# Decode backward, last pass: V and dS two blocks ahead of dV, dK and dQ

## The chip, the cores and the metric

One core of a Trainium2 chip runs the whole program in one launch. The metric is the device time of one execution in microseconds (us). A kernel's time is the median of several executions; beside it stands one execution that the hardware profiler recorded, and every duration below comes from that one.

## The reference

One token passes through four layers: attention over a cache of 65,536 keys and values (32 query heads in 4 groups of 8, head size 128), a feed-forward layer with squared ReLU, and both once more with the same weights and the same cache. The result and the gradients of all inputs but the feed-forward layer's own x are returned, so also the gradients of the K and V caches (4 x 65,536 x 128 each, bf16, 67 MB each).

```python
q = (x @ wq).reshape(...)                       # x: one token, layer-normed
scores = einsum("bhqd,bhkd->bhqk", q, k) * Dh ** -0.5
o = einsum("bhqk,bhkd->bhqd", softmax(scores), v)
A = o.reshape(...) @ wo                          # x = x + A(ln(x))
B = relu(ln(x) @ w1 + b1) ** 2 @ w2 + b2         # x = x + B
...
x = x + A(ln(x)); x = x + B(ln(x)); x = x + A(ln(x)); x = x + B(ln(x))
# returned: x and vjp(grad_out) for x, K, V, wq, wo, w1, b1, w2, b2
```

Both attention layers use the same K and V. So the gradient of one value row is a sum over two layers and eight heads, P^T dO, and that of a key row is dS^T q over the same sixteen pairs, where dS = P * (dO V^T - delta).

## The kernel before, in words

The caches are read in four passes: forward of layer 1, forward of layer 3, backward of layer 3 alone (dS and dQ), and a last pass, `attn_bwd4`, that works for both layers at once. Between the passes stand stages with the dense weights. The change concerns the last pass, which begins at about 1236 us of the profile and lasts to its end.

**Blocks and steps.** A block is 4096 keys of one head group as a tile of 128 partitions x 32 columns x 128 (`J` = 32): 1 MB in bf16. There are 64 blocks, 16 for each of the four groups. A step is an eighth of 64 columns, 8 columns of 128 keys; a block has four steps, the pass 256. `pipeline(items, stages, bg, end)` writes the steps out: in loop step i, a stage with lag l works on item i - l. In the last pass the order in which the engines get the instructions is not written out by hand: the framework's scheduler orders each engine's queue, with the order of the code as priority. Each engine then works through its queue in order.

**The stages of the last pass.** `vT` (lag 0) asks for the V block, transposes eight 128x128 pieces on TensorE (L1226) and copies them from PSUM (tile `kt`). The first seven V blocks were left in the arena, transposed, by the pass before and need neither. `vT` also copies the probabilities of both layers for the block into one tile, `xin`, on GpSimd (L1233). `vS` (lag 2) sets up a group or a unit of 128 columns (`g_setup`, `su_setup`), transposes `xin` (L1239), and forms dO V^T - delta in one PSUM tile (L1256 for delta, L1259 for the eight products). At the end of a block VectorE multiplies by the probabilities (X, L1267: this is dS), and TensorE transposes X at once (L1239). `dV8` (lag 3) makes the V gradient from the transposed probabilities, `k8` (lag 7) asks for the K block, adds K's part of dQ (L1306) and makes the K gradient from the transposed X. Both gradients go through `outer16`: pairs of TensorE products (L1280), a copy from PSUM into a slot (`evac`, L150 on ScalarE or L153 on VectorE, by estimated load), and a store from GpSimd's queue (L1286).

**Slots.** All K and V blocks, weight slabs and outgoing gradients live in the arena: 20 slots of 1 MB, of which 12 are free for this at the pass's start while 8 hold the probabilities of the four groups and two layers; two more come free when a group is done (`E_done`). Which slot each piece gets is fixed when the program is written out. For a load of the last pass, `take_one` picks

```python
early = [i for t, i in by_age if t <= NOW["step"] - AHEAD]   # AHEAD = 9
i = early[-1] if early else by_age[0][1]
```

and for an outgoing piece the youngest slot given back at least one step before. A stored slot counts as given back five steps later. Loads go out on the sync queue (L330 for K and V, L424 for weight slabs), which works in order and waits for each slot's last user.

**Around the steps.** `Background.step` runs one piece per step of the weight gradients (`g_outer`, `g_outer_wide`, products at L1345, stores at L1363), spread over the first 252 steps, and of the row products that give dO of the next group and the gradient of the layer's input (weight slabs of wo and wq, L549 and L540). The `end` list fetches the last V blocks and the last wq slabs at fixed distances from the loop's end. After the loop come the last group's row product and its part of dWq.

Of the kernel before, what the change touches and what calls it, by code (L numbers as in the profile page):

```python
# [10 lines left out]
BF = mybir.dt.bfloat16  # L11
# [5 lines left out]
P = 128  # L17
# [3 lines left out]
def kernel(  # L21
# [24 lines left out]
    nc = tc.nc  # L46
# [6 lines left out]
    R = HQ // G  # L53
# [3 lines left out]
    J = 32  # L57
    NB = C // J
    SU = min(128, C)
# [5 lines left out]
    R2, R4 = 2 * R, 4 * R  # L65
    TLEAD = 2
# [9 lines left out]
    tmp = ctx.enter_context(tc.tile_pool(name="tmp", bufs=2))  # L76
# [88 lines left out]

    def col_from_dram_f(v1d, n, name):
        nj = n // P
        rows = tmp.tile([nj // 4, 4 * P], BF, name="rows_f", tag="rows_f", bufs=1)
        nc.sync.dma_start(out=rows[:], in_=v1d.rearrange("(s x) -> s x", x=4 * P))
        pt = ps_mv([P, 4, 8], BF)  # L170
        col = vec.tile([P, nj // 4, 4], F32, name=name)
        for j in range(4):
            nc.tensor.transpose(pt[:, j, 0:nj // 4], f_cols(rows, j), ident_b[0:nj // 4, 0:nj // 4])
            nc.vector.tensor_copy(out=col[:, :, j], in_=pt[:, j, 0:nj // 4])
        return col[:, :, :].rearrange("p s j -> p (s j)")

    def col_to_dram_f(col, n, v1d):
        nj = n // P
        rows = tmp.tile([nj // 4, P, 4], BF, name="rows_f", tag="rows_f", bufs=1)
        c3 = col[:, :].rearrange("p (s j) -> p s j", j=4)  # L180
        for j in range(4):
            pt = ps_mv([nj // 4, P], F32)
            nc.tensor.transpose(pt[:, :], c3[:, :, j], ident_f[:, :])
            nc.vector.tensor_copy(out=rows[:, :, j], in_=pt[:])
        nc.gpsimd.dma_start(out=v1d.rearrange("(s x) -> s x", x=4 * P), in_=rows[:].rearrange("s p j -> s (p j)"))

    def col_to_dram(col, n, v1d):
        nj = n // P
# [184 lines left out]

    FWD_LAG = TLEAD + SU // 8 + 18
    B3_LAG = TLEAD + HB // 8 + 3
    B4_LAG = TLEAD + J // 8 + 1
    DV_LAG = TLEAD + 1
    ITEMS = [order_by_unit(False, SU), order_by_unit(True, SU), order_by_unit(False, HB), order_by_unit(True, J)]
    TOUCH = [touch_order(ITEMS[0], [("k", 0), ("v", FWD_LAG)]), touch_order(ITEMS[1], [("k", 0), ("v", FWD_LAG)]),
             touch_order(ITEMS[2], [("v", 0), ("k", B3_LAG)]), touch_order(ITEMS[3], [("v", 0), ("k", B4_LAG)])]  # L380
# [788 lines left out]
    def attn_bwd4(p, La, Lb, on_group, bg, stack, end=()):  # L1169
        dspool = stack.enter_context(tc.tile_pool(name="b4_ds", bufs=2))  # L1170
        items = ITEMS[p]
# [14 lines left out]
        def g_setup(g):  # L1186
            sl = gsl(g)
            for i, L in enumerate((La, Lb)):
                nc.vector.tensor_copy(out=DOB[:, g, 0, i * R:(i + 1) * R], in_=L["dOT"][:, sl])
                nc.vector.scalar_tensor_tensor(out=CCf[:, g, 0, i * R:(i + 1) * R], in0=L["qT"][:, sl], scalar=SCALE, in1=L["rZ"][:, sl],  # L1190
                                               op0=ALU.mult, op1=ALU.mult)
                nc.vector.tensor_tensor(out=CCf[:, g, 1, i * R:(i + 1) * R], in0=L["dOT"][:, sl], in1=L["rZ"][:, sl], op=ALU.mult)
            ndt = dspool.tile([64, J, R2], BF, name="ndt4", tag="ndt4", bufs=1)
            for i, L in enumerate((La, Lb)):
                nc.vector.tensor_copy(out=ndt[:, :, i * R:(i + 1) * R], in_=L["nd2"][:, sl].unsqueeze(1).to_broadcast([64, J, R]))
            state["ndt"] = ndt

        def su_setup(g, su):
# [19 lines left out]
        def vT(g, c8):  # L1218
            bg.need(g)
            vb8 = kv8("v", g, c8)  # L1220
            if is_turned("v", g, c8):
                state[("vt", g, c8)] = vb8
            else:
                pt = ps_tr()
                for i in range(8):
                    nc.tensor.transpose(pt[:, i, :], vb8[:, i, :], ident_b[:, :])  # L1226
                kv_done("v", g, c8)
                vt = turned_to("v", g, c8, vb8)
                evac(vt[:, :, :], pt[:, :, :])
                state[("vt", g, c8)] = vt  # L1230
            if c8 % J == 0:
                xin = dspool.tile([P, J, R2], BF, name="xin", tag="xin", bufs=1)
                nc.gpsimd.tensor_copy(out=split2(xin[:, :, :]), in_=E2(g, c8, J))  # L1233
                state[("xin", g, c8 // J)] = xin

        def x_transpose(src):
            pt = ps_tr()
            for bi in range(J // 8):
                nc.tensor.transpose(pt[:, bi, :], src[:, 8 * bi:8 * bi + 8, :].rearrange("p a b -> p (a b)"), ident_b[:, :])  # L1239
            xt = dspool.tile([P, J // 8, P], BF, name="xt", tag="xt", bufs=4)  # L1240
            evac(xt[:, :, :], pt[:, 0:J // 8, :])
            return xt

        def vS(g, c8):
            if c8 == gfirst[g]:
                g_setup(g)
            if c8 == sufirst[(g, c8 // SU)]:
                su_setup(g, c8 // SU)
            if c8 % J == 0:
                state[("xe", g, c8 // J)] = x_transpose(state.pop(("xin", g, c8 // J)))  # L1250
            vt = state.pop(("vt", g, c8))
            for i in range(8):
                s = (c8 + i) % J
                if s == 0:
                    state["ps_dp"] = ps_sc([P, J, R2])
                    nc.tensor.matmul(state["ps_dp"][:, :, :].rearrange("p c r -> p (c r)"), lhsT=sel2[:, :],  # L1256
                                     rhs=state["ndt"][:, :, :].rearrange("o c r -> o (c r)"), start=True, stop=False)
                w = min(4, J - s)
                nc.tensor.matmul(state["ps_dp"][:, s:s + w, :].rearrange("p a b -> p (a b)"), lhsT=vt[:, i, :],  # L1259
                                 rhs=DOB[:, g, 0:w, :].rearrange("p a b -> p (a b)"), start=False, stop=(s == J - 1))  # L1260
            if is_turned("v", g, c8):
                kv_done("v", g, c8)
            if (c8 + 8) % J == 0:
                c0 = c8 + 8 - J
                ps_dp = state["ps_dp"]
                X = dspool.tile([P, J, R2], BF, name="X", tag="X")
                nc.vector.tensor_tensor(out=split2(X[:, :, :]), in0=split2(ps_dp[:, :, :]), in1=E2(g, c0, J), op=ALU.mult)  # L1267
                add_load(dve=0.13 + J * R2 * 0.00105)
                state[("xd", g, c0 // J)] = (X, x_transpose(X[:, :, :]))
                E_done(g, c0, J)  # L1270

        def outer16(name, out, key, xt, gg, j1):

# [20 lines left out]
        def k8(g, c8):  # L1294
            kb8 = kv8("k", g, c8)
            b, j0 = divmod(c8, J)
            su = c8 // SU
            X, xt = state[("xd", g, b)]
            if c8 == sufirst[(g, su)]:
                state["ps_dq"] = ps_acc([P, 4, R2])  # L1300
            ps_dq = state["ps_dq"]
# [349 lines left out]
```

## Time and profile before

| | before |
|---|---|
| median of 4 runs | 2031.04 us (2027.91 to 2035.96) |
| the profiled execution | 2033.67 us, its span 2031.9 us |
| granted TensorE clock, mean | 0.901 |
| busy over the span: TensorE, its weight loads, VectorE, ScalarE, GpSimd | 81%, 66%, 58%, 51%, 7% |
| busy in the last pass (1250 to 2031.9, 781.90 us) | TensorE 647.69, weight loads 403.36, VectorE 547.17, ScalarE 518.71, GpSimd 134.01 us |
| DMA in the last pass (the same stretch) | 305.33 MB, mean 391 GB/s, share 0.96 |
| K and V blocks loaded there | 62 and 57, of 1 MB; from request to landing 17.5 and 18.2 us (median) |
| stores of 1 MB there | 150; 11.5 us to landing (median) |

The span runs from the first to the last instruction; the execution's own time is 1.8 us longer. "Share" of DMA is the mean busy share of the core's 16 DMA engines; it can read slightly above 1 in a short stretch, since a packet counts in the stretch in which it starts. A matmul's end is modelled, so a busy TensorE is not TensorE at its peak.

### The profile page before, as it was taken

The page shows a single profiled execution, that of the slowest core. Times are in us where ns is not written, and L with a number is a line of the kernel's source. Part 1 is how long each engine was busy: PE and PEld are TensorE (multiplying, and loading weights), DVE is VectorE, ACT ScalarE, POOL GpSimd, SP SyncE. Part 2 cuts the span into 40 slices and gives each one's busy share as a digit, 9 for nine tenths or more (in the row PEclk, how much of TensorE's full clock was granted, in tenths as well). Part 3 has the DMA queues.
Part 4 walks back from the last instruction along what each step waited for, and adds up shares of the span by engine and source line. Part 5 has one row for each costly group of instructions (what it writes and reads, how often), then busy time and mean ns, then how long its engine had stood idle before and what let it go on. Part 6 is the DMA issues. An engine that isn't in the chain of part 4 may idle for free. (4 is left out here: it accounts for less than half of the span.)

```text
span 2031.9 us, 67015 instructions
## 1 busy us (share of the span) xinstructions
PE 1636.3 (81%) x30210; PEld 1336.1 (66%) x30210; DVE 1175.4 (58%) x2358; ACT 1044.6 (51%) x1613; POOL 143.1 (7%) x332
## 2 busy tenths in 40 slices
PE   6878778687877787787787897888788888698896
PEld 6877777687777776786676795455455555455554
DVE  5645455245545543445354466577667776677675
ACT  3434344153343352435363355586667676677575
POOL 0000000000000000000000001111111111111111
PEclk9989899799999998898999988789888888898898
DMA  9999999999999997899999976899999999999996
GB/s 390 420 420 420 419 423 398 371 362 419 420 419 419 419 405 287 344 420 419 420 418 409 401 271 250 329 424 423 421 419 423 380 423 383 374 422 425 424 373 243
DMA packets 110845, 794.97 MB, mean 391 GB/s; under 512 B 9424, under 2 KB 9438, under 8 KB 49374
## 3 DMA queue, kind: packets, MB, share of 16 engines
q1 hardware_dynamic: 86510, 624.99, 75.5%
q0 software_dynamic: 24048, 165.70, 19.8%
q8 instruction: 236, 3.87, 0.8%
q14 instruction: 51, 0.42, 0.1%
HBM read 624.96 MB, written 165.69 MB: 389 GB/s over the span
## 5 line engine op out<-in xcount | busy, mean ns | idle before, releaser
L153 DVE COPY kt<-ps_tr 128x1024 bf16<-128x1024 bf16 x724 | 497.5, 689 | 476.8 <-PE ps_tr L913 252.8
L150 ACT CAST arena<-ps_gg 128x1024 bf16<-128x1024 f32 x452 | 439.9, 1009 | 223.5 <-PE ps_gg L1280 172.5
L913 PE MATMUL ps_tr<-ident_b,arena 128*128 128x128 bf16 x3840 | 309.0, 225 | 56.7 <-DMA arena<-in_A_k_cache_dram 42.3
L913 PEld LDWEIGHTS <-arena 128*128 128x128 bf16 x3840 | 233.0, 101 | 65.1 <-DMA arena<-in_A_k_cache_dram 44.8
L153 DVE CAST arena<-ps_gg 128x1024 bf16<-128x1024 f32 (+1 forms) x191 | 228.8, 1198 | 80.0 <-PE ps_gg L1280 45.5
L150 ACT COPY kt<-ps_tr 128x1024 bf16<-128x1024 bf16 x164 | 172.5, 1055 | 186.6 <-PE ps_tr L1105 126.5
L1280 PE MATMUL ps_gg<-GG,xt 64*128 64x512 bf16 x1024 | 215.4, 419 | 41.0 <-DVE arena L153 23.8
L1015 PE MATMUL ps_acc<-arena 128*128 128x64 bf16 (+4 forms) x4096 | 206.0, 196 | 48.5 <-DMA arena<-in_A_v_cache_dram 29.5
L1226 PE MATMUL ps_tr<-ident_b,arena 128*128 128x128 bf16 x1824 | 178.7, 236 | 42.6 <-DMA arena<-in_A_v_cache_dram 41.4
L931 PE MATMUL ps_sc<-L_qpad,kt 128*128 128x64 bf16 (+7 forms) x3584 | 183.8, 194 | 19.2 <-issue 13.6
L1105 PE MATMUL ps_tr<-ident_b,arena 128*128 128x128 bf16 x1920 | 157.6, 228 | 47.4 <-DMA arena<-in_A_v_cache_dram 46.2
L996 ACT ACTIVATE arena<-S_sb,L_negm 128x128 bf16<-128x128 f32 x256 | 165.6, 1003 | 56.9 <-DVE L_negm L981 56.9
L1015 PEld LDWEIGHTS <-arena 128*128 128x128 bf16 x4096 | 159.6, 100 | 50.7 <-DMA arena<-in_A_v_cache_dram 32.8
L1226 PEld LDWEIGHTS <-arena 128*128 128x128 bf16 x1824 | 121.1, 105 | 97.6 <-issue 51.1
L931 PEld LDWEIGHTS <-kt 128*128 128x128 bf16 x3584 | 153.3, 100 | 24.9 <-issue 16.2
L1105 PEld LDWEIGHTS <-arena 128*128 128x128 bf16 x1920 | 119.5, 103 | 50.9 <-DMA arena<-in_A_v_cache_dram 49.1
L1306 PE MATMUL ps_acc<-X,arena 128*128 128x64 bf16 (+3 forms) x2048 | 119.8, 199 | 17.0 <-DMA arena<-in_A_k_cache_dram 17.0
L996 ACT ACTIVATION_READ_ACCUMULATOR arena<-S_sb,L_negm 128x1 f32 x256 | 127.9, 500 | 0.0
L1306 PEld LDWEIGHTS <-arena 128*128 128x128 bf16 x2048 | 87.0, 102 | 53.0 <-issue 34.2
L1150 PE MATMUL ps_acc<-dsT,arena 128*128 128x64 bf16 (+7 forms) x2048 | 104.1, 196 | 18.9 <-DMA arena<-in_A_k_cache_dram 14.4
L1259 PE MATMUL ps_sc<-DOB,kt 128*128 128x64 bf16 (+3 forms) x1824 | 118.5, 200 | 0.0
L1259 PEld LDWEIGHTS <-kt 128*128 128x128 bf16 x1824 | 86.0, 103 | 49.1 <-issue 47.6
(266 smaller groups left out, 2149.4 us busy)
## 6 DMA issues: line engine op xcount, KB each, us to landing
arena<-in_A_k_cache_dram SPq DMA_DIRECT2D x86, 2048.0 KB, 21.5
arena<-in_A_v_cache_dram SPq DMA_DIRECT2D x83, 2048.0 KB, 21.5
out_dram<-arena POOLq DMA_DIRECT2D x151, 1024.0 KB, 11.5
arena<-in_A_v_cache_dram SPq DMA_DIRECT2D x76, 1024.0 KB, 18.0
arena<-in_A_k_cache_dram SPq DMA_DIRECT2D x76, 1024.0 KB, 17.2
arena<-in_B_w_dram SPq DMA_DIRECT2D x32, 896.0 KB, 5.8
arena<-in_A_wq_dram SPq DMA_DIRECT2D x22, 1024.0 KB, 13.4
arena<-in_A_wo_dram SPq DMA_DIRECT2D x18, 1024.0 KB, 17.2
```

The costliest lines, as they stand in the source:

```text
L150: nc.scalar.copy(out=out, in_=in_)
L153: nc.vector.tensor_copy(out=out, in_=in_)
L913: nc.tensor.transpose(pt[:, i, :], kb8[:, i, :], ident_b[:, :])
L931: nc.tensor.matmul(state["ps_s"][:, s:s + w, :].rearrange("p a b -> p (a b)"), lhsT=kt[:, i, :], rhs=L["qpad"][:, g, 0:w, :].rearrange("p ...
L996: nc.scalar.activation(out=E(p, g, c0, SU)[:, :, h], in_=S[:, h, :], func=ACTF.Exp, bias=L["negm"][:, g, su, h:h + 1], scale=SCALE, accum_ ...
L1015: nc.tensor.matmul(ps_o[:, 0:w, :], lhsT=vb8[:, i, :], rhs=E(p, g, c, w), start=(c % SU == 0), stop=(c % SU == SU - 1), skip_group_check=True)
L1105: nc.tensor.transpose(pt[:, i, :], vb8[:, i, :], ident_b[:, :])
L1150: nc.tensor.matmul(ps_dq[:, 0:w, :].rearrange("p a b -> p (a b)"), lhsT=kb8[:, i, :], rhs=dsT[:, s:s + w, :].rearrange("p a b -> p (a b)") ...
L1226: nc.tensor.transpose(pt[:, i, :], vb8[:, i, :], ident_b[:, :])
L1259: nc.tensor.matmul(state["ps_dp"][:, s:s + w, :].rearrange("p a b -> p (a b)"), lhsT=vt[:, i, :], rhs=DOB[:, g, 0:w, :].rearrange("p a b - ...
L1280: nc.tensor.matmul(pg[:, 512 * h:512 * h + 512], lhsT=xt[64 * h:64 * h + 64, j1 // 8 + m, :], rhs=gg[64 * h:64 * h + 64, :, :].rearrange(" ...
L1306: nc.tensor.matmul(ps_dq[:, 0:w, :].rearrange("p a b -> p (a b)"), lhsT=kb8[:, i, :], rhs=X[:, s:s + w, :].rearrange("p a b -> p (a b)"), ...
```

## The change

`V_AHEAD` = 8 steps, two blocks, is added to the lags of `dV8` (3 to 11) and `k8` (7 to 15); `vT` and `vS` keep theirs. The loop becomes 271 steps long. The copy of the probabilities to `xin` and their transposes leave `vT` and `vS` and become stages of their own, `eIn` (lag 8) and `eT` (lag 10), the latter with the set-up of a unit. X is no longer transposed when it is made but when `k8` starts on its block; it waits in one of four buffers instead of two. The probabilities' planes are given back in `eIn` of a group's last block. Three edits make room: the broadcast of -delta is read with a zero step instead of being written out (`ndt`, 16 values instead of 512 on each of 64 partitions), and the rows of the first feed-forward bias and of its gradient use an arena slot instead of a tile of their own.

```diff
     def col_from_dram_f(v1d, n, name):
         nj = n // P
-        rows = tmp.tile([nj // 4, 4 * P], BF, name="rows_f", tag="rows_f", bufs=1)
-        nc.sync.dma_start(out=rows[:], in_=v1d.rearrange("(s x) -> s x", x=4 * P))
+        sl = Slot("rows_f")
+        rows = sl.t[0:nj // 4, 0:4 * P]
+        nc.sync.dma_start(out=rows, in_=v1d.rearrange("(s x) -> s x", x=4 * P))
...
     def col_to_dram_f(col, n, v1d):
         nj = n // P
-        rows = tmp.tile([nj // 4, P, 4], BF, name="rows_f", tag="rows_f", bufs=1)
+        sl = Slot("rows_f", True)
+        rows = sl.t[0:nj // 4, 0:4 * P].rearrange("s (p j) -> s p j", j=4)
...
-    B4_LAG = TLEAD + J // 8 + 1
-    DV_LAG = TLEAD + 1
+    V_AHEAD = 2 * J // 8
+    B4_LAG = TLEAD + J // 8 + 1 + V_AHEAD
+    DV_LAG = TLEAD + 1 + V_AHEAD
...
-            ndt = dspool.tile([64, J, R2], BF, name="ndt4", tag="ndt4", bufs=1)
+            ndt = dspool.tile([64, R2], BF, name="ndt4", tag="ndt4")
             for i, L in enumerate((La, Lb)):
-                nc.vector.tensor_copy(out=ndt[:, :, i * R:(i + 1) * R], in_=L["nd2"][:, sl].unsqueeze(1).to_broadcast([64, J, R]))
+                nc.vector.tensor_copy(out=ndt[:, i * R:(i + 1) * R], in_=L["nd2"][:, sl])
...
         def vT(g, c8):
...
-            if c8 % J == 0:
-                xin = dspool.tile([P, J, R2], BF, name="xin", tag="xin", bufs=1)
-                nc.gpsimd.tensor_copy(out=split2(xin[:, :, :]), in_=E2(g, c8, J))
-                state[("xin", g, c8 // J)] = xin
...
         def vS(g, c8):
             if c8 == gfirst[g]:
                 g_setup(g)
-            if c8 == sufirst[(g, c8 // SU)]:
-                su_setup(g, c8 // SU)
-            if c8 % J == 0:
-                state[("xe", g, c8 // J)] = x_transpose(state.pop(("xin", g, c8 // J)))
...
-                                     rhs=state["ndt"][:, :, :].rearrange("o c r -> o (c r)"), start=True, stop=False)
+                                     rhs=state["ndt"][:, :].unsqueeze(1).to_broadcast([64, J, R2]), start=True, stop=False)
...
-                X = dspool.tile([P, J, R2], BF, name="X", tag="X")
+                X = dspool.tile([P, J, R2], BF, name="X", tag="X", bufs=2 + V_AHEAD * 8 // J)
                 nc.vector.tensor_tensor(out=split2(X[:, :, :]), in0=split2(ps_dp[:, :, :]), in1=E2(g, c0, J), op=ALU.mult)
                 add_load(dve=0.13 + J * R2 * 0.00105)
-                state[("xd", g, c0 // J)] = (X, x_transpose(X[:, :, :]))
-                E_done(g, c0, J)
+                state[("X", g, c0 // J)] = X
+
+        def eIn(g, c8):
+            if c8 % J == 0:
+                xin = dspool.tile([P, J, R2], BF, name="xin", tag="xin", bufs=1)
+                nc.gpsimd.tensor_copy(out=split2(xin[:, :, :]), in_=E2(g, c8, J))
+                state["xin"] = xin
+                E_done(g, c8, J)
+
+        def eT(g, c8):
+            if c8 == sufirst[(g, c8 // SU)]:
+                su_setup(g, c8 // SU)
+            if c8 % J == 0:
+                state[("xe", g, c8 // J)] = x_transpose(state["xin"])
...
         def k8(g, c8):
...
-            X, xt = state[("xd", g, b)]
+            X = state[("X", g, b)]
+            if j0 == 0:
+                state["xd"] = x_transpose(X)
+            xt = state["xd"]
...
-        pipeline(items, [(vT, 0), (vS, TLEAD), (dV8, DV_LAG), (k8, B4_LAG)], bg, end)
+        pipeline(items, [(vT, 0), (vS, TLEAD), (eIn, DV_LAG - 3), (eT, DV_LAG - 1), (dV8, DV_LAG), (k8, B4_LAG)], bg, end)
```

More of the change, by code (lines that the diff above doesn't have):

```diff
@@ L174, in col_from_dram_f @@
             nc.vector.tensor_copy(out=col[:, :, j], in_=pt[:, j, 0:nj // 4])
+        sl.free()
         return col[:, :, :].rearrange("p s j -> p (s j)")
@@ L184, in col_to_dram_f @@
             nc.vector.tensor_copy(out=rows[:, :, j], in_=pt[:])
-        nc.gpsimd.dma_start(out=v1d.rearrange("(s x) -> s x", x=4 * P), in_=rows[:].rearrange("s p j -> s (p j)"))
+        nc.gpsimd.dma_start(out=v1d.rearrange("(s x) -> s x", x=4 * P), in_=sl.t[0:nj // 4, 0:4 * P])
+        sl.free(stored=True)
     def col_to_dram(col, n, v1d):
```

## The prediction

> **What bounds the kernel now.** I read the page's slices first. The DMA row is at 9 tenths nearly everywhere; the change touches only the last pass, so I cut that pass into windows by how full the DMA engines are (columns: stretch, its length, busy time and instructions of each engine, granted TensorE clock, DMA share, GB/s).
>
> ```profile
> DMA  9999999999999997899999976899999999999996
> ...
> 1218.00:1241.00 23.00, 18.42 (x321) 16.06 (x318) 15.68 (x49) 11.62 (x15) 2.56 (x6) 0.88 0.67 248
> 1241.00:1250.00 9.00, 8.80 (x125) 5.19 (x122) 7.31 (x17) 6.44 (x7) 1.81 (x3) 0.93 0.29 118
> 1250.00:1260.00 10.00, 9.34 (x140) 5.65 (x138) 8.00 (x11) 7.43 (x8) 1.59 (x3) 1.00 0.67 213
> 1260.00:1280.00 20.00, 12.82 (x151) 7.41 (x148) 9.31 (x18) 7.57 (x8) 3.98 (x8) 0.66 0.97 381
> 1280.00:1300.00 20.00, 12.02 (x158) 7.34 (x158) 7.96 (x15) 9.33 (x10) 2.22 (x4) 0.75 0.93 364
> 1300.00:1320.00 20.00, 19.20 (x196) 11.49 (x195) 15.63 (x24) 11.62 (x13) 3.68 (x7) 0.74 0.83 287
> 1320.00:1580.00 260.00, 216.79 (x2732) 136.49 (x2732) 188.96 (x328) 183.50 (x222) 45.21 (x86) 0.88 1.01 422
> 1700.00:1760.00 60.00, 43.27 (x526) 27.02 (x523) 36.80 (x59) 36.21 (x49) 8.76 (x16) 0.78 0.92 360
> 1940.00:1985.00 45.00, 41.00 (x516) 25.52 (x516) 33.55 (x61) 32.04 (x36) 8.41 (x14) 0.92 0.94 357
> 1985.00:2003.00 18.00, 17.18 (x242) 11.16 (x239) 13.96 (x19) 13.22 (x14) 2.87 (x5) 1.00 0.94 383
> ```
>
> From 1320 to 1580 the DMA engines are full at 422 GB/s. There no reordering of TensorE's work can save time, because the bytes are the same. What is to be had lies where the share is below 1. By (1 - share) x length: at the pass's start 7.6 + 6.4 + 3.3 + 0.6 + 1.4 + 3.4 = 22.7 us; in 1700 to 1760 4.8 us; at the end, before the last block's K work is done, 2.7 + 1.1 = 3.8 us. After 2003 a serial chain follows (last dQ, its row product, the last part of dWq), which the change leaves as it is.
>
> Next, who waits: for TensorE and GpSimd in the whole pass, then for TensorE in its first 64 us, then the sync queue's own waits and its first loads.
>
> ```profile
> PE ps_tr L1226 <- DMA arena<-in_A_v_cache_dram: 41.4, 13, 7.6
> PEld L1239 <- DVE X L1267: 20.6, 45, 1.1
> POOL xin L1233 <- PE ps_tr L1239: 106.7, 41, 17.9
> ```
>
> ```profile
> PE ps_tr L1226 <- DMA arena<-in_A_v_cache_dram: 7.6, 1, 7.6
> PE ps_acc L1306 <- DMA arena<-in_A_k_cache_dram: 6.9, 1, 6.9
> ```
>
> ```profile
> SPq L330 <- DMA out_dram<-arena: 556.7, 95, 13.6
> SPq L330 <- PE ps_sc L1259: 37.1, 5, 26.5
> ```
>
> ```profile
> 1221.83 4.44 SPq L330 DMA_DIRECT2D arena<-in_A_k_cache_dram  x2
> ```
>
> ```profile
> 1252.85 4.73 SPq L330 DMA_DIRECT2D arena<-in_A_k_cache_dram  x2
> ```
>
> Loads wait for arena slots, and slots wait for stores (95 waits, 556.7 us). Only two K blocks are asked for before the pass begins; the next two follow 26.5 us later, and TensorE then stands 6.9 us for one of them. So the pass starts short of slots while the DMA engines idle.
>
> **The change part by part.**
>
> *Two blocks of V first.* The first seven V blocks of the pass are already in the arena, transposed. The loop grows from 263 to 271 steps: eight steps of V work alone at the front, eight without V at the back. Every load's slot is chosen when the code is written out: the youngest slot given back at least nine steps earlier, else the oldest. I followed that rule through both programs. Before, K0 (step 7) and K1 (step 11) get two of the five slots free at the start, dV0, dK0 and a background product take the other three, and K2 and K3 (steps 15, 19) get slots that a store and a V block must leave first. After, K0 to K3 (steps 15 to 27) get four slots that are empty when the pass starts. From step 28 on each load has the same step and, but for single cases, the same slot age as before (median 9 to 10 steps). So in the steady part DMA demand per step is identical, and I count 0 there.
>
> *The start, by DMA time.* 1 MB takes 1.049/0.424 = 2.47 us. K0's slot is that of the first of two Wo slabs, whose transposes end at 1231. In 1218 to 1241 the engines were busy 0.67 x 23 = 15.4 us; without the two K loads 10.5, and with four from 1231 on 20.4, so 2.6 us stay idle. Then nothing can move until the first store. Before, that is issued at 1245.7. Two V-only blocks cost TensorE 2 x (1.8 for 32 matmuls of L1259 + 0.6 for L1256) = 4.8 us, less what ran between them already; I put the first store at 1249: 8 us idle. From there to 1320 I take a share of 0.95, between the 0.91 of 1260 to 1320 and the 1.01 after: 3.5 us. Sum 14.1 against 22.7: **8.6 us less**. Bounds: 2 less (first store 4 us later still, share 0.91) and 12 less (share 1.0 at once). The 6.9 us wait for K2 goes with it; what is late next is V7, whose slot still comes from a store.
>
> *The end.* Eight steps without V or background work hold two blocks of K, dK, dV, dQ. By DMA one such block is 3 MB, 7.4 us. By TensorE it is, from the pass's groups by form, (112.1 + 12.1 + 11.3 + 10.8)/64 = 2.3 for L1306, 212.4/64 = 3.3 for L1280, (28.0 + 27.7)/64 = 0.9 for L1239, so 6.5 us. DMA stays the bound, and these bytes have left the front, where they were in the way: no cost beyond the sum above. The chain that ended last runs through V's transposes, X and dS's transposes of the last two blocks between 1989 and 1992, just ahead of the final dK; after the change those are long done. I take half of the 3.8 us idle there: **1.9 less**, bounds 0 and 3.8.
>
> *dS transposed at K.* TensorE no longer waits for X right after VectorE makes it (20.6 us before weight loads, some 8 of them before matmuls). Four transposes (0.9 us) and one copy (0.42 on VectorE, 0.59 on ScalarE) keep their number. They now stand two steps (about 6 us) ahead of dK's first product, where they had four; the copy is a tenth of that. Cover: a full DMA queue; without it, 8 us of gain at most and 0.6 x 64 = 38 us of loss if every copy were waited for. I take 0.
>
> *P's copy and transposes later.* `xin`'s copy on GpSimd (0.62 us x 64) moves with dV; the spacing from one copy to the transposes that free its one buffer, and its place among the dV and dK stores on GpSimd's queue, stay. Behind it still queue stores, and who waits for those is the sync queue. 0. The arena planes of a finished head group come free three steps later (three times 9 us, two slots of some 14); the stretch around those points is at share 1.01, so 0, at worst one such 9 us.
>
> *Small edits, one answer.* X has four buffers; the broadcast of -delta is read with a zero step by the 64 matmuls of L1256 (0.43 us each) instead of being written out (0.21 us twice per group); the bias gradient's rows sit in a slot, which at worst makes one copy wait for a store (0 to 11.5 us, once, on VectorE in a full stretch). 0.
>
> Sum: -8.6 - 1.9 = -10.5 us. The profiled execution took 2033.67 us for a span of 2031.9, 2.6 above the median of the four runs. I take the saving off the median: 2031.04 - 10.5 = **2020.5 us** (2023.2 for an execution like the profiled one). The own range of this case is 2015 to 2029.
>
> Two rules of the Trainium skill bear on this. The last window of the start, 1300 to 1320, has TensorE 96% busy at a clock of 0.74 and DMA at 0.83: a slow clock, left by the two waits, was the bound there. "TensorE: Matmul & The Clock Gate", section "What's actually happening", says that one idle window of about 3.4 us halves the clock and one busy window restores it; by that the two waits would cost an estimated 2 x 1.7 = 3.4 us, while the trace shows 0.66 to 0.75 for 60 us, and both waits gone would win more than I count. Against the change speaks "Perfetto Trace Analysis", section "Optimization Strategy": stages with different bounds gain from being interleaved, and this change separates V from K at both ends. The trace does show 1241 to 1250 as a TensorE stretch (8.80 of 9 us) beside a DMA share of 0.29; by the rule, the sum would be the slower rival's.
>
> **The rivals.**
>
> *Nothing to measure* (0.16). The first store comes so late that the start gains 2 us, and the end gives it back: 2029 to 2033. For it: same bytes, same slot ages from step 28. Against it: the two K loads that move into idle DMA time are 4.9 us by themselves.
>
> *Slower* (0.30). Place: the eight steps after the last V block. If K there waits for a slot, the slot for a store and the store for K's products, as the 556.7 us of waits suggest, a block takes the pass's average of 781.9/64 = 12.2 us and not 7.4: 2 x 4.8 = 9.6 more. With a start gain of 2 that is 2031 + 9.6 - 2 = 2039, with none 2041. It decides once a block there takes more than 7.4 + gain/2: 12.7 us with my gains, 8.4 with the lowest start gain. Against it: slots for the last K loads were given back far more than nine steps before, and 6.5 us of TensorE fits under 7.4.
>
> *Much faster* (0.12). With V two blocks ahead its 13 waits (41.4 us) shrink and the dip of 1700 to 1760 fills too: 12 + 3.8 + 4.8 = 20.6, so 2010. Against it: V's load keeps its distance from its transposes in steps, and in the full stretches those waits cost nothing.
>
> **How the numbers follow.** The forecast has 0.42. What a measurement can tell from no change is 0.3%, 6 us. Faster: 0.38 of the forecast and 0.12, together 0.50. Within: 0.04 of the forecast, 0.16, and 0.02 of the slower case, 0.22. Slower: 0.28. The range runs from the fast rival's 2010 to the slow one's upper end, 2041.
>
> **What would show it.** Right: four K loads asked for between 1230 and 1241; DMA share near 0.9 there, near 0 for some 8 us after, near 1 from 1250; no wait of L1306 for K2; no wait of L1239 for X; the middle unchanged at 1.01 and 422 GB/s; about two blocks at 7 to 8 us between the last V product and the last dQ. Wrong: a share below 0.9 over the last 40 us before the final chain, new waits of TensorE on K or on `xt`, or a middle whose share falls.

## The result, and the profile after

| | before | after |
|---|---|---|
| median | 2030.17 us (2023.95 to 2035.96, 60 runs) | 2037.12 us (2029.41 to 2045.65, 38 runs) |
| ratio to before | | 1.0031, 95% interval 1.0024 to 1.0039 |
| the profiled execution, its span | 2033.67, 2031.9 us | 2044.16, 2042.4 us |
| first product of the pass to the end | 792.8 us | 803.8 us |
| TensorE's wait for K in the pass | 17.0 us, 3 times | 39.9 us, 9 times |
| from the last dQ product to the end | 25.7 us | 43.9 us |

The change costs 6 to 7 us where 10.5 us less were forecast: the "slower" rival, at a smaller price. The profiled execution of after lies 7 us above its median, that of before 3.5, so some 4 of the 11 us between the two profiles are spread between executions. The slices and the windows of after, to be laid beside those of before:

```profile
DMA  9999999999999997899999976999999999999985
```

```profile
1218.00:1241.00 23.00, 18.28 (x327) 16.07 (x324) 16.04 (x52) 10.60 (x13) 1.71 (x5) 0.88 0.92 343
1241.00:1250.00 9.00, 9.00 (x90) 4.57 (x88) 3.86 (x12) 5.31 (x6) 1.20 (x2) 0.50 0.14 61
1250.00:1260.00 10.00, 9.68 (x129) 5.75 (x127) 7.71 (x14) 6.63 (x8) 2.30 (x4) 0.87 0.39 159
1260.00:1280.00 20.00, 18.70 (x279) 11.73 (x277) 17.68 (x28) 14.63 (x16) 4.37 (x9) 1.00 0.97 373
...
1320.00:1580.00 260.00, 211.14 (x2720) 135.71 (x2718) 182.57 (x327) 177.70 (x216) 44.89 (x84) 0.86 0.99 409
...
1940.00:1985.00 45.00, 42.29 (x531) 25.88 (x529) 31.89 (x60) 33.83 (x37) 8.16 (x14) 0.90 0.83 318
1985.00:2003.00 18.00, 8.27 (x62) 3.61 (x60) 7.23 (x13) 5.98 (x6) 2.42 (x4) 0.54 0.76 278
2003.00:2042.00 39.00, 22.89 (x213) 11.92 (x212) 20.48 (x35) 18.55 (x20) 4.63 (x8) 0.68 0.47 189
```

The first window went from a DMA share of 0.67 to 0.92. The third last column is the clock; in the last three rows DMA is at 0.83, 0.76 and 0.47 where before had 0.94 and 0.94 up to 2003 and then only the serial chain. TensorE is 94% busy up to 1985 and then idles 9.7 of 18 us. The waits of TensorE, of VectorE and of the sync queue over the pass say for what:

```profile
PE ps_tr L1231 <- DMA arena<-in_A_v_cache_dram: 41.3, 10, 11.2
PE ps_acc L1318 <- DMA arena<-in_A_k_cache_dram: 39.9, 9, 12.4
PE ps_sc L1253 <- DVE X L1264: 18.0, 3, 11.3
```

```profile
DVE X L1264 <- DMA arena<-in_A_wq_dram: 18.8, 2, 11.4
```

```profile
SPq L334 <- DMA out_dram<-arena: 544.1, 97, 14.4
```

V's waits are as before; K's have more than doubled, and there is a new wait for X, which on VectorE itself waits for the load of a wq slab (why, i1 shows below). The load queue still waits for stores, 97 times.

Two profiles of one execution each are best compared by what bounds the pass. I counted the DMA bytes from 18 us before the pass's first product and read when 40, 250 and 304 MB had moved; the time from the first product, less these bytes at 423.5 GB/s (about the rate of the fullest stretch, 423 from 1320 to 1480 in before), is DMA time lost. The last column but one is the whole time from there to the end.

| us lost | first 40 MB | 40 to 250 | 250 to 304 | 304 MB to the end | pass |
|---|---|---|---|---|---|
| before | 13.4 | 17.0 | 7.6 | 37.0 | 792.8 |
| after | 5.4 | 17.6 | 23.0 | 40.0 | 803.8 |
| difference | -8.0 | +0.6 | +15.4 | +3.0 | +11.0 |
| forecast | -8.6 | 0 | -1.9 | 0 | -10.5 |

So start and middle came as forecast, and the end did not.

### The profile page after: what moved, and what is told of

Same layout as the page of the kernel before. It is cut to its first block, busy times and chain, and to the rows that moved or that the text cites. A ratio compares the mean times of both kernels' runs of the same rounds, so it can differ in the third digit from the quotient of the medians.

```text
span 2042.4 us, 66994 instructions
## 1 busy us (share of the span) xinstructions
PE 1623.3 (79%) x30210; PEld 1334.9 (65%) x30210; DVE 1166.3 (57%) x2364; ACT 1043.1 (51%) x1607; POOL 144.7 (7%) x332
## 5 line engine op out<-in xcount | busy, mean ns | idle before, releaser
L150 ACT CAST arena<-ps_gg 128x1024 bf16<-128x1024 f32 (+1 forms) x455 | 443.3, 1012 | 229.7 <-PE ps_gg L1289 187.1
L153 DVE CAST arena<-ps_gg 128x1024 bf16<-128x1024 f32 (+1 forms) x188 | 223.9, 1191 | 65.7 <-PE ps_gg L1289 40.5
L1289 PE MATMUL ps_gg<-GG,xt 64*128 64x512 bf16 x1024 | 211.2, 415 | 34.2 <-DVE arena L153 16.3
L1231 PE MATMUL ps_tr<-ident_b,arena 128*128 128x128 bf16 x1824 | 177.4, 232 | 43.4 <-DMA arena<-in_A_v_cache_dram 41.3
L936 PE MATMUL ps_sc<-L_qpad,kt 128*128 128x64 bf16 (+7 forms) x3584 | 184.2, 194 | 16.8 <-issue 10.9
L1318 PE MATMUL ps_acc<-X,arena 128*128 128x64 bf16 (+3 forms) x2048 | 128.7, 199 | 39.9 <-DMA arena<-in_A_k_cache_dram 39.9
L1289 PEld LDWEIGHTS <-xt 64*128 64x128 bf16 x1024 | 64.4, 94 | 76.7 <-issue 40.4
## 6 DMA issues: line engine op xcount, KB each, us to landing
arena<-in_A_wq_dram SPq DMA_DIRECT2D x22, 1024.0 KB, 14.7
arena<-in_A_wo_dram SPq DMA_DIRECT2D x18, 1024.0 KB, 16.8
```

What stands on the lines that cost most here:

```text
L150: nc.scalar.copy(out=out, in_=in_)
L153: nc.vector.tensor_copy(out=out, in_=in_)
L936: nc.tensor.matmul(state["ps_s"][:, s:s + w, :].rearrange("p a b -> p (a b)"), lhsT=kt[:, i, :], rhs=L["qpad"][:, g, 0:w, :].rearrange("p ...
L1289: nc.tensor.matmul(pg[:, 512 * h:512 * h + 512], lhsT=xt[64 * h:64 * h + 64, j1 // 8 + m, :], rhs=gg[64 * h:64 * h + 64, :, :].rearrange(" ...
L1318: nc.tensor.matmul(ps_dq[:, 0:w, :].rearrange("p a b -> p (a b)"), lhsT=kb8[:, i, :], rhs=X[:, s:s + w, :].rearrange("p a b -> p (a b)"), ...
```

## The experiments

Every ratio is to the kernel before on the same chip, with its 95% interval; before's medians there were 2029.4 to 2031.4 us.

**How far V runs ahead.** Theory: the end's loss comes with V's distance. Rival: the rest of the change (dS transposed with K, P's copy later) costs it.

```diff
-    V_AHEAD = 2 * J // 8
+    V_AHEAD = 0            # e1_ahead0; J // 8 in e2_ahead4
```

> The changed kernel with V_AHEAD = 0: V as near as before, but dS transposed when its K arrives, the copy and transposes of the probabilities in stages of their own, the two bias rows in a slot. Slot theory (the pass now ends in two more blocks without V, whose K loads come too late because each waits for a slot whose store landed shortly before; TensorE stands for K63 with gradient products queued behind it) and copy theory (those blocks run at the pace of the copies out of ps_gg, 8 per block at 0.9 to 1.1 us, and the last row product and dWq queue behind them): the tail is as before, so 2030 us, within 3. Reordering theory (the moved transposes and copies make new waits, the distance of V does not matter): it keeps the loss, 2036.

> The changed kernel with V one block ahead (V_AHEAD = 4) instead of two. Slot and copy theory: half of the gain at the start (about 4 us) and half of the loss at the end (about 8 us): 2033 to 2034. Reordering theory: as the changed kernel, 2036.

e1: 2028.45 us, 0.9987 (0.9972 to 1.0001). With no distance the last X block of a group is made from probability planes that are already given back, so a part of dK there is computed from other data; the work is the same, and the planes come free five steps earlier than in the kernel before. e2: 2028.32 us, 0.9987 (0.9971 to 1.0004), where 2033 to 2034 was expected: a miss. The rest of the change, taken together, costs nothing, so the loss belongs to the distance; but it is not in proportion to it.

**Which slot K's loads take.** Theory: the youngest slot that is nine steps old ties a K load to a store that has hardly left. Rival: the end is bound by other work.

```diff
-            i = early[-1] if early else by_age[0][1]
+            i = early[-1] if early and not NOW.get("last") else by_age[0][1]
...
     def last_v():
+        NOW["last"] = True     # e3 in after, e4 in before, f4 with V_AHEAD = 4
...
+            i = early[-1] if early and load != "k" else by_age[0][1]      # f2: for every K load
```

> The changed kernel, but after the last V load has been asked for, each K load takes the free slot that was given back longest ago instead of the youngest of at least nine steps. Slot theory: the last K blocks are asked for early, the 7.1 us wait for K63 and the 4.1 us one before go, and the pass ends 7 to 15 us earlier: 2022 to 2030. Copy theory and reordering theory: no change, 2036 within 2.

> The kernel before with the same rule for the last K loads. Slot theory: its tail has no wait for K of over 1.5 us, so 0 to 3 us less, 2027 to 2030. Copy theory: 2030.

> The kernel with V ahead, and every K load of the last pass takes the slot given back longest ago instead of the youngest that is nine steps old. Theory: TensorE's waits for K (39.9 us in nine waits with V ahead, 17.0 in three before) come from slots given back too lately, so they fall below 15 us; if they cost time outside the end as well, 2020 to 2026. Rival: in the stretches where the DMA engines are full such waits cost nothing, only the end gains, and it is as fast as with the rule for the last K loads alone, 2027. Second rival: V loads are left with the younger slots, TensorE waits for V instead (41.3 us now), and the time is 2030 or more.

> V one block ahead (4 steps) instead of two, with the oldest-slot rule for the K loads after the last V load. Slot theory: the end of one K-only block still loses 2 to 4 us to late K loads, which the rule gives back: 2024 to 2026 beside 2028 without it. Rival: with one block ahead the last K slots were already free in time, nothing changes, 2028.

e3: 2027.35 us, 0.9986 (0.9965 to 1.0008), 0.45% below after. e4: 2031.01 us, 1.0007 (0.9992 to 1.0021): nothing, where 0 to 3 less were expected. f2: 2024.94 us, 0.9971 (0.9959 to 0.9983), 0.6% below after, and the first version below before. Its waits over the pass:

```profile
PE ps_tr L1231 <- DMA arena<-in_A_v_cache_dram: 68.2, 15, 14.2
PE ps_acc L1318 <- DMA arena<-in_A_k_cache_dram: 16.5, 2, 11.7
```

K's waits fall from 39.9 to 16.5 us (below 15 was expected), V's rise from 41.3 to 68.2, and the middle still loses no more DMA time than in after (15.5 us from 40 to 250 MB, 17.6 in after); in 250 to 304 MB the kernel loses 14.6 us and not 23.0. But f4: 2035.47 us, 1.0026 (1.0015 to 1.0038), 7 us slower than the same kernel without the rule, where 2 to 4 less were expected. TensorE's, VectorE's and ScalarE's queues are the same there, only the last forty or so loads stand in another order and slots. In e3 and f2 the new slots change the order too: that of the loads and, by the scheduler, that of TensorE's queue (in e3 in its tail, in f2 over much of the pass). So the rule is not good in itself: it mends this order, and another one it spoils.

**The start alone.**

```diff
         start_pass(p)
+        for g, c8 in items[0:3 * J // 8:J // 8]:     # 4 * J // 8 in g2
+            kv8("k", g, c8)
```

> The kernel before, with the loads of the first three K blocks asked for at the start of the pass, ahead of its first step, and nothing else changed. It tests the start term alone: the DMA engines idle 22.7 us in the first 100 us of the pass, and a K load put there moves 2.47 us of transfer into idle time. Theory (idle DMA time at the start can be won without V ahead, up to two blocks more than now): 3 to 5 us less, 2026 to 2028 beside 2031. Rival (the slots they take are then missing for dV and V, the gain is given back): 2030 to 2032.

> The kernel before, with four K blocks instead of three asked for ahead of the pass. With three, 14.8 us of DMA time (23 x 0.39, 9 x 0.41 and 70 x 0.03) are still idle in 1218 to 1320. Start theory: one more block, 2.47 us of transfer, goes into idle time: 2018 to 2020 beside 2021 with three. Rival (the slot it takes is missing for the first V gradients and background stores, which then wait): 2021 to 2024.

> The kernel before, with three K blocks asked for ahead of the pass and the oldest free slot for every K load. With V two blocks ahead that rule brought the time from 2037 to 2025. Theory (the rule mends a shortage that only the two K-only blocks and their distance bring): without V ahead it brings 0 to 2 us, 2019 to 2021 beside 2021. Rival (the youngest-slot rule makes K late in any order): 2014 to 2018. Second rival (V loads are left with younger slots and come late): 2023 or more.

f3, the kernel before with its first three K blocks asked for ahead of the pass: 2021.01 us, 0.9954 (0.9940 to 0.9969). The idle DMA time at the start can be had without V ahead, and 9 us of it reach the end. g2, with a fourth: 2030.00 us, 0.9998 (0.9986 to 1.0010); the rival was right, and more so than it said. The first three windows of f3 and of g2:

```profile
1218.00:1241.00 23.00, 17.54 (x313) 13.44 (x310) 16.88 (x54) 12.01 (x15) 3.85 (x8) 1.00 0.61 240
1241.00:1250.00 9.00, 8.73 (x134) 5.34 (x131) 6.75 (x9) 6.95 (x8) 2.21 (x4) 1.00 0.59 204
1250.00:1320.00 70.00, 55.26 (x659) 33.05 (x658) 44.43 (x73) 40.61 (x46) 12.77 (x25) 0.83 0.97 378
```

```profile
1218.00:1241.00 23.00, 17.39 (x316) 13.81 (x313) 16.44 (x55) 11.64 (x14) 3.25 (x7) 1.00 0.76 300
1241.00:1250.00 9.00, 7.90 (x168) 6.10 (x166) 4.50 (x6) 3.52 (x4) 1.81 (x3) 1.00 0.29 118
1250.00:1320.00 70.00, 55.54 (x596) 31.76 (x595) 43.65 (x69) 39.97 (x44) 12.03 (x24) 0.73 0.89 340
```

g2's fourth block fills the first window (0.76 against 0.61) and empties the second and third: in 1218 to 1320 it moves 0.89 x 70 + 0.29 x 9 + 0.76 x 23 = 82.4 us of DMA time, f3 87.2. g3 (f3 with the oldest slot for every K load): 2030.78 us, 1.0004 (0.9989 to 1.0019), 10 us worse; its profiled execution, 2022.8 us, lies 8 below its median, so that profile does not tell where.

**What paces the end.** Three tries on the gradients' copies, after the profile of after had shown them late:

```diff
-            if 2 * j0 >= J:
+            if 2 * j0 >= J and (g, b // 2) != (0, 0):     # f1, on e3
...
+                if both:                                   # g1, on f2: last two blocks
+                    nc.scalar.copy(out=stg[:, jj:jj + 4, :]..., in_=pg[:, 0:512])
+                    nc.vector.tensor_copy(out=stg[:, jj + 4:jj + 8, :]..., in_=pg[:, 512:1024])
...
-    DV_LAG = TLEAD + 1 + V_AHEAD
+    DV_LAG = TLEAD + 1                                     # g4, on f2 (E_done back in vS)
```

> The kernel with V ahead and the oldest-slot rule for the K loads after the last V load, with one part left out: the K gradients of the last two blocks are not computed (16 product groups' worth of TensorE work, 8 copies out of PSUM, 2 stores of 1 MB). It asks what bounds the stretch after the last V block. Theory A (the copies out of the gradients' PSUM tile, 0.9 to 1.1 us each, pace it): 8 copies less, 7 to 9 us less, so 2018 to 2021 beside 2027 for the same kernel with the gradients. Theory B (DMA paces it): 2 MB less, 4.9 us, 2022. Theory C (the late K loads pace it, stores and copies lie beside them): 0 to 2 us less, 2025 to 2027.

> The kernel with V ahead and the oldest slot for every K load; the 16 copies out of the gradients' PSUM tile that belong to the last two blocks (V and K gradients) are each made as two halves, one on ScalarE and one on VectorE at the same time. Nothing else changes. Theory A (after the last V block the pace is set by filling and emptying the two buffers of that tile): a copy takes about half of its 1.0 to 1.1 us, so 3 to 6 us less, 2019 to 2022 beside 2025 without it. Theory B (the pace there is set by the loads and stores): nothing changes, 2024 to 2026.

> The kernel with the oldest slot for every K load, but only the K stages (dQ, dK and dS's transposes) run two blocks behind V; the V gradient keeps its old distance of three steps. After the last V block a block then holds 4 copies and 2 MB (one load, one store: 4.9 us of DMA) instead of 8 copies and 3 MB. Theory (the end is too dense for its eight steps, in copies and stores): 4 to 8 us less than with the V gradient behind as well, 2017 to 2021. Rival (the start's gain came from the V gradient's later stores, which left slots free): 2024 to 2030.

f1: 2023.77 us, 0.9969 (0.9952 to 0.9986) against e3's 0.9986 (0.9965 to 1.0008): some 3.5 us with intervals that overlap, between the theories. g1: 2025.51 us, 0.9976 (0.9960 to 0.9993), nothing; but it tried nothing, as its stretch after the last dQ shows:

```profile
1986.46 0.58 ACT L1294 CAST arena<-ps_gg 128x512 bf16<-128x512 f32 x1 [0.48 <-PE ps_gg L1289]
...
1987.07 0.69 DVE L1295 CAST arena<-ps_gg 128x512 bf16<-128x512 f32 x1 [0.25 <-ACT arena L1294]
```

VectorE's half starts only when ScalarE's is done: 0.58 + 0.69 is no less than one copy of 1.0 to 1.2 us. g4: 2026.40 us, 0.9990 (0.9979 to 1.0000): its end loses less (11.0 us in 250 to 304 MB, against f2's 14.6), its start more (12.1 in the first 40 MB, against 5.7). So the gain of the start goes when the V gradient does not run behind as well, as the rival said.

**Where the last row product stands.** After the last dQ (2006.2 before, 1998.5 after) TensorE has this left, before and then after:

```profile
L1280 PE MATMUL ps_gg<-GG,xt 64*128 64x512 bf16 x4 | 1.1, 384 | 0.9 <-ACT arena L150 0.9
```

```profile
L1289 PE MATMUL ps_gg<-GG,xt 64*128 64x512 bf16 x38 | 8.9, 486 | 4.3 <-DVE arena L153 2.3 <-ACT arena L150 1.9
L636 PE MATMUL ps_tr<-ident_b,arena 128*128 128x128 bf16 x64 | 6.6, 252 | 0.1
```

Before, 4 gradient products and none of the 64 weight transposes of the last row product; after, 38 and all 64. dWq's last part takes its PSUM tiles behind those gradients, and from the last gradient store to the end it is 19.7 us in both. And this is what TensorE did just ahead, in order of time:

```profile
1987.30 1.10 PE L1289 MATMUL ps_gg<-GG,xt 64*128 64x512 bf16 x4
1995.54 1.09 PE L1318 MATMUL ps_acc<-X,arena 128*128 128x64 bf16 x17 [7.14 <-DMA arena<-in_A_k_cache_dram]
```

It stood 7.1 us for the last K block, whose load was issued at 1986.7, while the slab for those transposes had been there since 1838 and the transposes stood behind in its queue. `fill4` and the slab's load are counted from the loop's end, which had moved eight steps away from the last V block. Theory: counted from V they fill that wait.

```diff
-    ... (12, pre_load("wq4", ...)), (5, fill4)])
+    ... (12 + V_AHEAD, pre_load("wq4", ...)), (5 + V_AHEAD, fill4)])   # h1 on after, h2 on f2; 20 and 13 in h4 on before
...
+        LATE.append(lambda: outer16(*args))      # h3, on h2: last two blocks' gradients, run after run(gwq(...))
```

> The changed kernel, and only the last row product's slab loads and its 64 weight transposes are written eight steps earlier (the distance from the loop's end grows from 12 to 20 and from 5 to 13), so that they keep their distance from the last V block. Theory (V ahead lengthened the loop behind V, and the row product, tied to the loop's end, came to stand behind the last dQ with 38 gradient products): its transposes then fill the waits for the last K blocks; 7 to 12 us less than the changed kernel, 2025 to 2030. Rival (TensorE is busy there anyway, so the transposes only delay dQ): 0 to 3 us less, 2034 to 2037.

> The same move of the row product on top of the oldest-slot rule for all K loads (2025 without the move). Theory: the last gradient copies end 5 to 12 us sooner, 2013 to 2020. Rival (what remains after the last dQ is bound by the gradients' copies, 46 products or 11.5 tiles at 1.05 us, and the row product lay beside them): 2023 to 2026.

> As the kernel with the row product early and the oldest-slot rule, and the V and K gradients of the last two blocks (16 tiles) are written behind the last part of dWq instead of ahead of it. Theory (the gradients' tiles, taken in the order of the code, hold back dWq's last part by about 1 us each, and the 20 us from there to the end leave TensorE idle enough for them): dWq ends 10 to 16 us sooner, but the last gradient store then comes 16 tiles, 17 us, after it and lands 11 us later: 2010 to 2020. Rival (the two queues only change places): 2020 to 2026.

> Control: the kernel before, with the last row product's slab loads and transposes eight steps earlier (20 and 13 steps from the loop's end). There the transposes already ran just ahead of the last dQ (1998.6 to 2006.0 of the profile, the last dQ at 2006.2) while TensorE was full. Theory: no gain, 2028 to 2032. Rival (an early row product helps in any order): 2020 to 2025.

h1: 2033.42 us, 1.0011 (0.9998 to 1.0023), 4 us below after; the order of the loads is the same, and TensorE's queue differs in the tail alone. h2: 2022.38 us, 0.9960 (0.9946 to 0.9973), 2 to 3 us below f2, with intervals that overlap. h4: 2030.05 us, 0.9998 (0.9989 to 1.0006), nothing, as expected. The place of the row product costs something, due to the longer loop: some 4 us by h1, and not 7 to 12. h3: 2026.31 us, 0.9979 (0.9965 to 0.9993): putting the gradients last only changes who comes last. In h1 the transposes run here:

```profile
L636 PE MATMUL ps_tr<-ident_b,arena x64: 216/219/229, 1986.8 to 1995.0; 128*128 128x128 bf16 x64
```

Its last dQ is at 1990.5, and the gradients still end at 2010.3: 20 us for 38 products.

**The last two runs.** More PSUM for the gradients at the end (a proper trial of what g1 missed), and one block ahead with everything that helped at two.

```diff
+                if tail and m == 1:                       # i2, on h2: every second tile of the last two blocks
+                    for h in range(2):
+                        pq = ps_sc([P, 512])
...
+    V_AHEAD = J // 8                                      # i1, on h2
```

> The kernel with the oldest slot for every K load and the row product early; of the 16 gradient tiles of the last two blocks, every second one is made as two halves in the PSUM buffer that V's products no longer need then, so that the other two buffers turn over half as often. Theory A (the turn-over of two buffers, 1.0 to 1.8 us for a tile and its copy, paces the end): 3 to 6 us less, 2016 to 2019 beside 2022. Theory B (loads, stores or TensorE's own order pace it): 2021 to 2024.

> The oldest-slot rule for all K loads and the row product's distance kept to the last V block, with V one block ahead instead of two. Theory: the gradient products behind the last V block go from 80 to about 56 and the end costs some 7 us less, but by the profile of V one block ahead the DMA time lost by the first 60 MB is 15.4 us and not 5.4, so the start's gain goes too: 2024 to 2029 beside 2022 with two blocks. Rival (the end weighs more than the start): 2014 to 2020.

i2: 2022.76 us, 0.9962 (0.9947 to 0.9977): the same as h2, so the 3 to 6 us of theory A are not seen. It is a weak trial: the added buffer is one, and the second half of each tile waits there until the first is copied. i1: 2048.12 us, 1.0098 (1.0080 to 1.0116), 26 us above h2, where 2 to 7 were expected. Its waits of VectorE, then of TensorE:

```profile
DVE X L1264 <- DMA arena<-in_A_wq_dram: 25.1, 2, 17.0
DVE X L1264 <- DMA arena<-in_A_wo_dram: 23.4, 1, 23.4
```

```profile
PE ps_sc L1253 <- DVE X L1264: 47.4, 5, 22.5
```

X itself waits for the load of a weight slab that it does not read, and TensorE for X, 47.4 us in all; in after it was 18.0, in f2 5.4, in before nothing. X reads the two probability planes of its group, four slots apart, in one strided access. In the programs as built just these X (two in after, three in i1) are ordered behind a load, and each time it is that of a slab whose slot, 14 or 15, lies between the two planes. The slab loads are in the same queue as K and V, behind loads that wait for stores. Such waits alone need not make a kernel slow: TensorE waits 16.1 us for X in e1 and 12.6 in e2. No theory of mine had that.

The lost DMA time of the kernels that the reading rests on (each profile is one execution: e3's lies 7.9 us below its kernel's median, e2's 7.3 above, f2's 2.3 above, h2's 2.3 below, those of i1 and f3 within 1):

| us lost | first 40 MB | 40 to 250 | 250 to 304 | to the end |
|---|---|---|---|---|
| after, oldest slot for the last K (e3) | 0.9 | 14.7 | 15.9 | 36.0 |
| after, oldest slot for all K (f2) | 5.7 | 15.5 | 14.6 | 35.8 |
| the same, row product early (h2) | 0.1 | 14.2 | 16.8 | 34.8 |
| one block ahead (e2) | 11.1 | 27.9 | 7.0 | 34.7 |
| one block ahead, all edits (i1) | 9.7 | 21.4 | 24.8 | 35.2 |
| before, three K blocks early (f3) | 5.2 | 20.8 | 4.5 | 38.4 |

## Why the prediction was wrong

*The start, right.* 8.6 us less were forecast, and after loses 8.0 less in its first 40 MB. The order of events came as written, the numbers nearly so: the four K loads left at once,

```profile
1225.97 7.20 SPq L334 DMA_DIRECT2D arena<-in_A_k_cache_dram  x4
```

the last at 1233 (forecast 1230 to 1241), then the DMA engines all but stood (0.14), and the wait for K2 is gone. What I had as "near 1 from 1250" came 10 us later (0.39 up to 1260), and a 12.4 us wait for K4 took K2's place. The 8.0 is from one execution each: e3 and h1 have the start of after and lose 0.9 and 1.9 us there, e4 and h4 that of before and lose 12.2 and 10.8, so by these six profiles the gain is about 9. Every kernel with V two blocks ahead and the V gradient behind loses 0.1 to 5.7 us there, the others 9.7 to 13.5 unless K is asked for early. f3 shows that the term was a fair price for this time: 9 us at the end of the run.

*The middle, right.* 0 forecast, 0.6 measured from 40 to 250 MB. The dS transposes moved to K and the other small edits cost nothing either (e1).

*The end, wrong, and the sign with it.* "DMA stays the bound ... no cost beyond the sum above" and 1.9 less were forecast; 15.4 more were lost before the last bytes and 3.0 after. Three steps failed.

First, the argument against the slower rival: "slots for the last K loads were given back far more than nine steps before". I had the rule right and did not follow it to its last load. Followed again, that load takes the slot of a stored V gradient that counts as given back ten steps before. But a slot ten steps old is what the last K load gets in the kernel before, in e1 and in e2 too, and these lose nothing. I had taken equal ages in steps for equal ages in time, and at the end of after the same steps pass faster. The last K loads of before, then the very last of after:

```profile
1960.24 19.64 SPq L330 DMA_DIRECT2D arena<-in_A_k_cache_dram  x3
```

```profile
1986.69 0.33 SPq L334 DMA_DIRECT2D arena<-in_A_k_cache_dram  x1
```

Before, the last one left at 1979.6, 22 us ahead of its block's first product (2001.4). After, it left 1.7 us ahead of the moment at which TensorE came to its block (1988.4), and TensorE stood 7.1 us. With the oldest slot it leaves at 1933.6 (e3), TensorE's waits for K from 1860 on fall from 20.8 to 8.2 us, and the time is 10 (last loads, e3) to 12 us (all K loads, f2) lower. How much of that is the slot and how much the changed order is not shown. The rival's mechanism was the right one, "K there waits for a slot, the slot for a store". Its condition, 12.7 us a block with the gains of the forecast, is met only if the gradients are counted in: from the last V product (1977.1) there are 21.6 us to the last dQ, 10.8 a block, and 44.3 to the last gradient product. Its price of 9.6 us was too low (7 us slower in the medians in spite of 8 won at the start makes 15), and it was set against a start gain of 0 to 2 where 8 was there; the two errors nearly cancel, so it is luck that the time came out at 2037, just below its 2039 to 2041.

Second, "DMA stays the bound", at 7.4 us for a block against 6.5 us of TensorE. From the last V product to the last gradient product there are 13.7 us in before, 44.3 in after and 27.5 in h2, where TensorE waits for no K after 1900. TensorE has 18, 64 and 58 gradient products in that stretch, where the sum had 32 for two blocks: it left out what earlier blocks still owed, and the copies out of PSUM altogether. The stretch in h2:

```profile
1970.30:1997.80 27.50, 24.08 (x277) 13.72 (x275) 21.11 (x39) 20.98 (x22) 5.61 (x10) 0.92 0.70 282
```

DMA is at 0.70 there, and TensorE is busy 24.1 of 27.5 us.

Third, "a serial chain follows ..., which the change leaves as it is". After the last dQ it is 43.9 us and not 25.7. The list of things that are counted from the loop's end was in front of me, and I did not ask what a longer loop does to them. h1 prices the place of the row product at 4 us, h4 shows that nothing is to be had from it in the kernel before.

Slots and row product together bring 2037.1 to 2022.4 us (h2), near the 2020.5 forecast. I do not call that a proof of the whole sum. In 250 to 304 MB h2 still loses 16.8 us where before loses 7.6, 9 more, and no edit here took that away. What paces that rest stays open: leaving out the last two blocks' K gradients is worth some 3.5 us, not clear of the noise (f1), another PSUM buffer nothing that can be seen (i2). And other orders and slots of the loads, in f4, g2, g3 and i1, cost 7 to 26 us that no count of mine foretold (in i1, X's wait for a slab is one way); a part of what I put down to the slot rule may be such an accident of order.

Of the rules drawn on in the prediction, the Trainium skill's "Perfetto Trace Analysis", section "Optimization Strategy", advises to interleave stages with different bounds; this change parts V from K at both ends, and the trace agrees with it at the end: TensorE 42.29 of 45 us busy beside a DMA share of 0.83, then TensorE 8.27 of 18 beside 0.76. Before had 41.00 of 45 and 17.18 of 18, both beside 0.94.

f3 (2021.0 us) and h2 (2022.4) are both below the kernel before, by 0.46% and 0.40%. The first leaves V where it was.

## What to carry to other kernels

Before you lengthen one stage's lead, list everything that is counted from the loop's end or start, and follow the buffer rule to the last load and not only through the steady part, in time and not in steps: a slot ten steps old was early enough for the last load before and too late after. The end is where a lead has to be paid back. Where one access spans several buffers, ask what else lands between them. Where one resource bounds most of the time, compare two traces by the time lost at the same number of bytes moved; it shows at once which stretch gained and which gave back, and it keeps a start gain from being read as a whole gain. Idle transfer time at the start can be filled by asking for a few loads earlier, but not for any number: a third load was worth 9 us here, a fourth took it all back, with the DMA share in the window after it at 0.29 and not 0.59.

## What the hardware showed that I had not expected

TensorE ran at half its clock while it was busy without a break. The windows of after at the pass's start:

```profile
1236.00:1240.00 4.00, 2.58 (x43) 2.03 (x44) 3.51 (x19) 1.05 (x2) 1.48 (x5) 0.88 1.01 416
1240.00:1244.00 4.00, 4.00 (x37) 1.89 (x35) 3.16 (x8) 1.50 (x2) 0.62 (x1) 0.50 0.13 47
1244.00:1248.00 4.00, 4.00 (x42) 1.99 (x40) 1.59 (x6) 2.69 (x3) 0.36 (x1) 0.50 0.00 0
1248.00:1252.00 4.00, 4.00 (x50) 2.53 (x47) 1.71 (x4) 2.31 (x4) 0.84 (x2) 0.50 0.65 266
```

One window at 2.58 of 4 us busy was followed by 12 us at 0.50 with TensorE full. The Trainium skill's "TensorE: Matmul & The Clock Gate", section "What's actually happening", has the clock come back after about one busy window of 3.4 us; here it took more than three. The length differs from execution to execution: f2 and h2 have the same program at this place, and f2 stays at 0.50 to 0.52 for 12 us, h2 at 0.50 for 4. The kernel before dips to 0.72 in 1240 to 1244, TensorE 3.88 of 4 us busy, and is at 1.00 in the next 4 us. What sets the length is not shown.

The spread between executions of one kernel is wide and differs by kernel: 16 us for after (38 runs), 20 for e3 (12 runs), 7 for f2 (11 runs), 6 for f3 (6 runs), with the same bytes in each.
